# Spreading reciprocal denominators to rows by 32-row products in four parts of the array

## The chip, the cores and the metric

The kernel runs on one core of a Trainium2 chip. The metric is the device time of one execution in microseconds (us). Every time below is from the profile, its trace or the timed runs.

## What is computed

Four layers act on x, 2048 tokens of 576 numbers: linear attention (A), a feed-forward block (B), and the same two again with the same weights. Each adds its result to x. The change is in the attention layer, which has 32 heads of 18 numbers:

```
q, k, v = layernorm(x) @ wqkv, split by head
pq, pk  = phi(q), phi(k)          # phi(t) = t + 1 if t > 0 else exp(t), plus 1e-6
kv      = sum over tokens of pk (outer) v      # per head 18 x 18
z       = sum over tokens of pk                # per head 18
den     = pq . z + 1e-6                        # one number per token and head
o       = (pq @ kv) / den
x       = x + concat(o) @ wo
```

The B block is `gelu(layernorm(x) @ w1 + b1) @ w2 + b2` with 4608 hidden numbers.

## The kernel before

**Units.** Tokens stand in 16 tiles of 128 (`NT`), for the attention in 4 chunks (`NCA`) of 512 tokens (`CA`), four tiles each. The 32 heads stand in 5 groups (`G`): four of 7 heads, 126 rows, and one of 4 heads, 72 rows. `pq[(g, c)]` is phi(q) of group g and chunk c, turned: rows are the head's numbers, columns are 512 tokens.

**The attention layer (`layer_A`)** first makes the sums over all tokens, and among them queries by `q_proj` (L586), five products of 512 columns each (L589) into one PSUM buffer, which ScalarE reads twice (Exp L468, Identity L469) and VectorE completes (L476, L480). Three of the 20 `q_proj` are left for the passes 0, 1 and 2 of the output loop in layer 0, one for pass 0 in layer 2. `kv_wo` (L733) multiplies kv into wo.

**Denominators.** `den_stage(c)` (L748) makes the denominators of a chunk by products of 128 columns in four column parts of the array: rows 32j to 32j + 31 of the result are the 32 heads for tokens 128j to 128j + 127 (L755; the 1e-6 by L759). VectorE takes the reciprocal (L763) into `rden`, a single buffer. `quad_stage(c)` (L768) spreads `rden` on VectorE to `quad_rden`, 128 x 512, with a mask that leaves in each 128 columns only their own 32 rows.

**Scaling.** `scale_stage(g, c)` (L778) brings the reciprocals of a group to its rows by one product with all 128 rows and 512 columns (L783: `head_bc[:, g, :]`, a 0/1 matrix that repeats each head 18 times). ScalarE copies the result to bf16 (L785, `rden_bc`), VectorE multiplies it into `pq` (L786). The 0/1 matrix holds the same pattern once in each 32 rows.

**The output loop (L830)** runs over the 16 tiles t = 4c + j; one run of it is called a pass here. Its order is the order of TensorE, since the helper `pe` chains every product to the one before:

1. `wo_stage(t)` (L790): ten products (L795, 288 columns) of the scaled `pq` of chunk c into an accumulator pair, `accA` or `accB` in turn; VectorE adds the residual (`residual`, L519), which frees the pair for the pass after next.
2. `quad_stage` of a chunk whose reciprocal is due, and a `q_proj` if one is left.
3. `scale_stage` for the next chunk: groups 0 to 2 at j = 0, groups 3 and 4 at j = 1.
4. `den_stage(c + 2)` at j = 1.
5. `lnp.tick()`: the pipeline of row statistics for the first four tiles of the next block, on ScalarE (L337, L344) and GpSimd; from pass 6 on every second pass it transposes one of these tiles on TensorE (`tp`, L425), with a copy by ScalarE (L432).

The first chunk is scaled before the loop.

**Buffers.** PSUM has the two accumulator pairs and the pool `ps_h` of four banks. `q_proj`, `den_stage` (but for chunk 1), `scale_stage` and the transposes take their banks from `ps_h`, one each; a bank is free again when its readers are done. `turned` (L114) is an SBUF tile, 128 x 2304 in bf16, for rows on their way to be turned for the feed-forward block and, at its end, for the second attention layer; the output loop does not use it.

On ScalarE, VectorE and GpSimd the order is that of a scheduler, which mostly follows the program's, with some steps that are ready early put forward.

Of the kernel before, what the change touches and what calls it, by code (L numbers as in the profile page):

```python
# [8 lines left out]
ALU = mybir.AluOpType  # L9
BF16 = mybir.dt.bfloat16  # L10
F32 = mybir.dt.float32
# [4 lines left out]
P = 128  # L16
# [12 lines left out]
CA = 512  # L29
NCA = S // CA  # L30
# [4 lines left out]
def build(tc, A_x, A_wqkv, A_wo, B_w1, B_b1, B_w2, B_b2, out, dbg=None, n_layers=4):  # L35
    nc = tc.nc
    dbg = dbg or {}
    with ExitStack() as ctx:
        const = ctx.enter_context(tc.tile_pool(name="const", bufs=1))
        ps_h = ctx.enter_context(tc.tile_pool(name="ps_h", bufs=4, space=PSUM))  # L40
# [18 lines left out]
        head_bc = const.tile([P, G, P], BF16, name="head_bc")  # L59
# [54 lines left out]
        turned = const.tile([P, D // 32, TPC, 32], BF16, name="turned")  # L114
# [6 lines left out]
        rows = ctx.enter_context(tc.tile_pool(name="rows", bufs=9))  # L121
# [20 lines left out]
        def pe(inst):  # L142
            if pe_chain["on"]:
                if pe_chain["last"] is not None:
                    tc.add_manual_dep(inst.ins, pe_chain["last"], NOSYNC, reason="TensorE order in the MLP")
                pe_chain["last"] = inst.ins.name
            return inst
# [76 lines left out]
        dve_last = dict(norm=None, sum=None, phi=None)  # L224
# [222 lines left out]
        act_last = dict(exp=None, gelu=None)  # L447
# [14 lines left out]
        def phi_from_psum(ps_ap, out_ap, rows, n, turned_cols=False, after=None, dve_after=None, ident_after=None):  # L462
            e = work.tile([P, 512], BF16, name="phi_e", bufs=3)
            a = work.tile([P, 512], BF16, name="phi_a", bufs=2)
            e_out, a_out = e[0:rows, 0:n], a[0:rows, 0:n]
            if turned_cols:
                e_out, a_out, ps_ap = spread(e_out), spread(a_out), gather(ps_ap)
            exp = nc.scalar.activation(out=e_out, in_=ps_ap, func=ACT.Exp)  # L468
            ident_pass = nc.scalar.activation(out=a_out, in_=ps_ap, func=ACT.Identity, bias=C1, scale=1.0)  # L469
            if after is not None:  # L470
                for step in (exp, ident_pass):
                    tc.add_manual_dep(step.ins, after, NOSYNC, reason="broadcasts first")
            if ident_after is not None:
                tc.add_manual_dep(ident_pass.ins, ident_after, NOSYNC, reason="first rows first")
            act_last["exp"], act_last["phi"] = exp.ins.name, ident_pass.ins.name
            low = nc.vector.tensor_scalar(out=e[0:rows, 0:n], in0=e[0:rows, 0:n], scalar1=1.0, scalar2=1e-6,  # L476
                                          op0=ALU.min, op1=ALU.add)
            if ident_after is not None:
                tc.add_manual_dep(low.ins, dve_last["turned"], NOSYNC, reason="first rows first")
            top = nc.vector.tensor_tensor(out=out_ap, in0=a[0:rows, 0:n], in1=e[0:rows, 0:n], op=ALU.max)  # L480
            if dve_after is not None:
                tc.add_manual_dep(top.ins, dve_after, NOSYNC, reason="denominators first")
            dve_last["phi"] = top.ins.name
# [45 lines left out]
        def layer_A(li, next_kind, pre_a1=None):  # L529
# [3 lines left out]
            pq = {}  # L533
# [52 lines left out]
            def q_proj(g, c, defer=False):  # L586
                qp = ps_h.tile([P, 512], F32, name="q_ps", tag="h")
                for k in range(KD):
                    pe(nc.tensor.matmul(qp[0:GR[g], :], lhsT=wqkv_sb[:, k, GO[g]:GO[g] + GR[g]],  # L589
                                     rhs=yT[:, k, c * CA:(c + 1) * CA],  # L590
                                     start=(k == 0), stop=(k == KD - 1)))
                pq[(g, c)] = blk.tile([P, D], BF16, name="pq", tag="blk")
                phi = lambda after=None, dve_after=None: phi_from_psum(qp[0:GR[g], :], pq[(g, c)][0:GR[g], 0:CA], GR[g], CA,
                                                       turned_cols=(li > 0), after=after, dve_after=dve_after)
                if defer:
                    return phi
                phi()
# [4 lines left out]
            if li > 0:  # L602
# [87 lines left out]
                for g in range(G):  # L690
                    pe(nc.tensor.matmul(zp[0:GR[g], g:g + 1], lhsT=k2[4][:, GO[g]:GO[g] + GR[g]], rhs=ident[:, 64:65],
                                        start=True, stop=True))
# [30 lines left out]
            if li == 0:  # L723
# [5 lines left out]
                                    in1=zp[0:126, 0:4].unsqueeze(2).to_broadcast([126, 4, H]), op=ALU.mult)  # L729
            nc.vector.tensor_tensor(out=zsel[0:72, 4, :], in0=head_sel[0:72, 4, :],  # L730
                                    in1=zp[0:72, 4:5].to_broadcast([72, H]), op=ALU.mult)
# [12 lines left out]

            quad_rden = {}
            rden_of = {}

            def den_stage(c, after=None, pair=None):  # L748
                if pair:
                    dp = ps_acc.tile([P, 2, 512], F32, name="den_pair", tag=pair)[:, 0, :]  # L750
                else:
                    dp = ps_h.tile([P, 512], F32, name="den_ps", tag="h")
                for g in range(G):
                    for j in range(TPC):
                        pe(nc.tensor.matmul(dp[32 * j:32 * (j + 1), 0:P], lhsT=zsel[0:GR[g], g, :],  # L755
                                         rhs=pq[(g, c)][0:GR[g], j * P:(j + 1) * P],
                                         start=(g == 0), stop=False))
                for j in range(TPC):
                    pe(nc.tensor.matmul(dp[32 * j:32 * (j + 1), 0:P], lhsT=eps_row[:], rhs=one_row[:],  # L759
                                        start=False, stop=True))  # L760
                rden = work.tile([P, P], BF16, name="rden", bufs=1)
                with nc.allow_low_precision("reciprocal of the denominator in the reference's bfloat16"):
                    recip = nc.vector.reciprocal(out=rden[:], in_=dp[:, 0:P])  # L763
                if after is not None:
                    tc.add_manual_dep(recip.ins, after, NOSYNC, reason="first products first")
                rden_of[c] = rden

            def quad_stage(c, after=None):  # L768
                quad = blk.tile([P, D], BF16, name="quad_rden", tag="blk")
                spread_out = nc.vector.tensor_tensor(  # L770
                    out=quad[:, 0:CA].rearrange("p (j n) -> p j n", j=4), in0=quad_mask[:],
                    in1=rden_of.pop(c)[:].unsqueeze(1).to_broadcast([P, 4, P]), op=ALU.mult)
                if after is not None:
                    tc.add_manual_dep(spread_out.ins, after, NOSYNC, reason="sums first")
                quad_rden[c] = quad
                dve_last["quad"] = spread_out.ins.name

            def scale_stage(g, c, pair=None):  # L778
                if pair:
                    bp = ps_acc.tile([P, 2, 512], F32, name="rden_pair", tag=pair)[:, 0, :]  # L780
                else:
                    bp = ps_h.tile([P, 512], F32, name="rden_ps", tag="h")
                pe(nc.tensor.matmul(bp[:, 0:CA], lhsT=head_bc[:, g, :], rhs=quad_rden[c][:, 0:CA], start=True, stop=True))  # L783
                rb = blk.tile([P, D], BF16, name="rden_bc", tag="blk")
                act_last["copy"] = nc.scalar.copy(out=rb[0:GR[g], 0:CA], in_=bp[0:GR[g], :]).ins.name  # L785
                mult = nc.vector.tensor_tensor(out=pq[(g, c)][0:GR[g], 0:CA], in0=pq[(g, c)][0:GR[g], 0:CA],  # L786
                                               in1=rb[0:GR[g], 0:CA], op=ALU.mult)
                dve_last["mult"] = mult.ins.name

            def wo_stage(t):  # L790
                c, j = divmod(t, TPC)
# [28 lines left out]
            for g in range(3):  # L820
                scale_stage(g, 0)
# [8 lines left out]
            for t in range(NT):  # L830
                c, j = divmod(t, TPC)
                if t + AHEAD < NT:
                    prefetch_xo(li, t + AHEAD, add_b2=False)
                wo_stage(t)
                for late in list(rden_of):
                    quad_stage(late, after=dve_last["sum"])
                if q_left:
                    q_proj(*q_left.pop(0))
                if c + 1 < NCA:
                    for g in ((0, 1, 2), (3, 4), (), ())[j]:  # L840
                        scale_stage(g, c + 1)
                if j == 1 and c + 2 < NCA:
                    den_stage(c + 2)
                if t == NT - 3:
                    warm_table(ACT.Gelu_apprx_tanh, act_last["copy"])
                state["wo"] = t
                lnp.tick()
                if t < 10:
                    lnp.tick(transposes=0)
# [236 lines left out]
```

## Time and profile before

| what | value |
|---|---|
| median of 3 runs | 768.68 us (768.55 to 768.87) |
| the profiled execution | 768.49 us, span of its instructions 766.8 us |
| granted TensorE clock | 1.0 |
| output loop, layer 0 | from 77.69 to 107.2 us of the span |
| output loop, layer 2 | from 454.07 to 481.8 us of the span |
| L783, products that spread reciprocals | 40, one lasts 379 ns (median) |
| L785, copies of them by ScalarE | 40, 592 ns |
| L786, products on VectorE | 40, 417 ns |

How to read it: the profile holds one execution. PE is TensorE's products, PEld its weight loads, DVE is VectorE, ACT is ScalarE, POOL is GpSimd, SP starts transfers. L783 is line 783 of the kernel. A duration of a product is longer than the time after which the next may start, since they are pipelined; so starts are compared. The span is 1.7 us shorter than the time of its execution (768.49 less 766.8), and the execution 0.2 us faster than the median.

### The profile page before, as it was taken

What the parts mean: (1) busy time and instruction counts of PE and PEld (TensorE: products, weight loads), DVE (VectorE), ACT (ScalarE), POOL (GpSimd) and SP (SyncE); (2) the same over time, 40 slices, a digit from 0 to 9 for tenths busy, and PEclk for the clock granted to TensorE, in tenths of its full rate; (3) what the DMA queues carried; (4) which work ended last, traced back from release to release, by engine and by line L of the source; (5) the groups of instructions that cost most, each with busy time, mean ns of one, the idle gap of its engine ahead of it and who ended that gap; (6) DMA issues with size and microseconds to landing.
All of it is one profiled execution on the core that took longest, in us unless ns stands there. A gap on an engine that the chain in (4) does not pass through costs nothing.

```text
span 766.8 us, 15710 instructions
## 1 busy us (share of the span) xinstructions
PE 760.5 (99%) x6554; PEld 492.8 (64%) x6554; DVE 273.3 (36%) x677; ACT 338.6 (44%) x754; POOL 120.5 (16%) x196
## 2 busy tenths in 40 slices
PE   9999999999999999999999999999999999999998
PEld 6776664675477457646777767447745764674476
DVE  7786864135113603400355677600140032000000
ACT  5887856304610650164056567560065027205600
POOL 4571412011100301200100005300020021001000
PEclk9999999999999999999999999999999999999999
DMA  8992483016402721330256006630141033011000
GB/s 257 263 308 48 140 283 77 24 55 162 125 24 63 195 68 42 96 86 1 67 137 204 1 17 224 226 82 15 50 111 47 16 125 82 9 32 55 2 9 24
DMA packets 80289, 73.82 MB, mean 96 GB/s; under 512 B 36698, under 2 KB 64858, under 8 KB 80218
## 3 DMA queue, kind: packets, MB, share of 16 engines
q1 hardware_dynamic: 80218, 72.82, 32.7%
q8 instruction: 51, 0.84, 0.5%
q14 instruction: 20, 0.16, 0.1%
HBM read 48.03 MB, written 24.77 MB: 95 GB/s over the span
## 4 chain that ended last, share of the span: by engine, by line
PE 95%; ACT 3%; DVE 1%; DMA 1%; issue 1%; SPq 0%; DVEq 0%; ACTq 0%
PE m_ps L967 36%; PE h_ps L910 20%; PE hp_ps L910 16%; PE q_ps L589 5%; PE wo_ps L795 3%; PE k_ps L541 3%; PE k_ps L610 3%; PE k_ps L627 2%; PE v_ps L562 1%; PE m_half L967 1%; PE v_ps L559 1%; ACT rden_bc L785 1%; PE tp L425 1%; DMA wqkv_sb<-in_A_wqkv_dram 1%; ACT ln_dump L337 1%; PE kvacc L583 1%
## 5 line engine op out<-in xcount | busy, mean ns | idle before, releaser
L967 PE MATMUL m_ps<-w_sb,hT 128*128 128x288 bf16 x2232 | 274.8, 286 | 0.0
L967 PEld LDWEIGHTS <-hT 128*128 128x128 bf16 x2304 | 224.8, 98 | 59.8 <-issue 3.4
L910 PEld LDWEIGHTS <-w_sb 64*128 64x128 bf16 x2304 | 124.5, 94 | 136.5 <-issue 1.9
L910 PE MATMUL hp_ps<-yT,w_sb 64*128 64x512 bf16 x1152 | 178.0, 376 | 0.0
L910 PE MATMUL h_ps<-yT,w_sb 64*128 64x512 bf16 x1152 | 147.9, 376 | 0.0
L915 ACT COPY relay_sb<-relay_sb 128x1 f32<-128x1 f32 x144 | 28.5, 198 | 262.6 <-PE h_ps L910 220.0
L906 ACT ACTIVATE hT<-h_ps,b1T 128x512 bf16<-128x512 f32 x144 | 91.0, 683 | 44.4 <-PE h_ps L910 44.4
L376 POOL TENSOR_TENSOR ln_rstd<-ln_u,neg_half 128x1 f32<-128x1 f32 x64 | 36.2, 566 | 379.0 <-DVE ln_u L367 230.7
L906 ACT ACTIVATE hT<-hp_ps,b1T 128x512 bf16<-128x512 f32 x144 | 91.1, 692 | 0.0
L519 DVE TENSOR_TENSOR xbf<-m_ps,xo 128x576 bf16<-128x576 f32 x15 | 11.4, 757 | 214.0 <-PE m_ps L967 214.0
L519 DVE TENSOR_TENSOR xo<-m_ps,xo 128x576 f32<-128x576 f32 x16 | 12.1, 758 | 173.8 <-PE m_ps L967 173.8
L502 POOL TENSOR_TENSOR xo<-xo,b_bc 128x576 f32<-128x576 f32 x32 | 40.9, 1284 | 102.0 <-DMA xo<-x_d 61.9
L910 PE MATMUL h_ps<-yT,w_tail 64*128 64x512 bf16 x144 | 54.1, 376 | 0.0
L910 PE MATMUL hp_ps<-yT,w_tail 64*128 64x512 bf16 x144 | 54.1, 376 | 0.0
L589 PE MATMUL q_ps<-yT,wqkv_sb 128*126 128x512 bf16 (+1 forms) x200 | 49.8, 380 | 0.0
L795 PE MATMUL wo_ps<-kvwo,pq 126*128 126x288 bf16 (+1 forms) x320 | 43.7, 286 | 0.6 <-DVE xo L519 0.2
L910 PEld LDWEIGHTS <-w_tail 64*128 64x128 bf16 x288 | 27.1, 94 | 17.1
L795 PEld LDWEIGHTS <-pq 126*128 126x128 bf16 (+1 forms) x320 | 30.1, 97 | 11.1 <-DVE pq L786 0.8
L468 ACT ACTIVATE phi_e<-k_ps 128x288 bf16<-128x288 f32 x46 | 19.4, 421 | 38.2 <-PE k_ps L610 35.5
L468 ACT ACTIVATE phi_e<-q_ps 126x512 bf16<-126x512 f32 (+1 forms) x40 | 23.8, 596 | 19.0 <-PE q_ps L589 19.0
L589 PEld LDWEIGHTS <-wqkv_sb 128*126 128x126 bf16 (+1 forms) x200 | 24.9, 131 | 11.4
L476 DVE TENSOR_SCALAR phi_e<-phi_e 128x288 bf16<-128x288 bf16 (+2 forms) x86 | 24.1, 281 | 21.0 <-ACT phi_e L468 20.3
(135 smaller groups left out, 665.5 us busy)
## 6 DMA issues: line engine op xcount, KB each, us to landing
xo<-x_d SPq DMA_DIRECT2D x48, 288.0 KB
x_d<-xo SPq DMA_DIRECT2D x32, 288.0 KB
xl<-x_d SPq DMA_DIRECT2D x24, 288.0 KB
y_d<-turned SPq DMA_DIRECT2D x40, 144.0 KB
w_sb<-in_B_w_dram SPq DMA_DIRECT2D x6, 864.0 KB
yT<-y_d SPq DMA_DIRECT2D x10, 512.0 KB
w_sb<-in_B_w_dram SPq DMA_DIRECT2D x9, 512.0 KB
x_d<-xn SPq DMA_DIRECT2D x16, 288.0 KB
```

What stands on the lines that cost most here:

```text
L376: nc.gpsimd.tensor_tensor(out=rstd[:], in0=it["u"][:], in1=neg_half[:], op=ALU.pow)
L468: exp = nc.scalar.activation(out=e_out, in_=ps_ap, func=ACT.Exp)
L476: low = nc.vector.tensor_scalar(out=e[0:rows, 0:n], in0=e[0:rows, 0:n], scalar1=1.0, scalar2=1e-6, op0=ALU.min, op1=ALU.add)
L502: nc.gpsimd.tensor_tensor(out=xo[:], in0=xo[:], in1=b2_bc[:], op=ALU.add)
L519: total = nc.vector.tensor_tensor(out=xn[:, cols].rearrange("p (h n) -> p h n", h=2), in0=halves, in1=xo[:, cols].rearrange("p (h n) -> p ...
L541: pe(nc.tensor.matmul(kp[:, 0:HALF], lhsT=yT[:, k, tok], rhs=wqkv_sb[:, k, D + half * HALF: D + (half + 1) * HALF], start=(k == 0), stop=( ...
L589: pe(nc.tensor.matmul(qp[0:GR[g], :], lhsT=wqkv_sb[:, k, GO[g]:GO[g] + GR[g]], rhs=yT[:, k, c * CA:(c + 1) * CA], start=(k == 0), stop=(k ...
L795: pe(nc.tensor.matmul(wp[:, half, 0:HALF], lhsT=pq[(g, c)][0:GR[g], j * P:(j + 1) * P], rhs=kvwo[g][0:GR[g], half * HALF:(half + 1) * HALF ...
L906: act_last["gelu"] = nc.scalar.activation(out=to, in_=ps, func=ACT.Gelu_apprx_tanh, bias=b1T[:, f:f + 1], scale=1.0).ins.name
L910: mm = pe(nc.tensor.matmul(dst[n], lhsT=wt, rhs=mv, start=(seen[n] == 0), stop=(seen[n] == 8)))
L915: relay = nc.scalar.copy(out=relay_sb[:, 1:2], in_=relay_sb[:, 0:1])
L967: pe(nc.tensor.matmul(acc[half][:, 0:HALF], lhsT=hT[f][:, j * P:(j + 1) * P], rhs=w2_sb[:, f, half * HALF:(half + 1) * HALF], start=(f == ...
```

## The change

For the chunks 1 to 3, groups 0 to 3 are no longer scaled one by one. A new `quarter_stage(c)` takes four banks of `ps_h`, one for each 128 tokens. For each group it makes four products, one for each 32 rows of `rden` and of the 0/1 matrix (126 of its columns), each into its own bank: 16 products of 32 rows and 128 columns in place of 4 of 128 rows and 512 columns. ScalarE copies each bank whole (four groups for 128 tokens) into a quarter of `turned`; VectorE multiplies group by group, and its second operand is then four runs of 128 columns, one from each bank's copy.

Group 4 keeps `scale_stage`, and with it `quad_stage` stays. In the loop the quarter stage stands at j = 0, but at j = 1 for chunk 1 (c = 0); group 4 and `den_stage(c + 2)` follow one pass later. Chunk 0 is not touched.

```diff
             rden_of = {}
+            rden_now = {}
...
                 rden_of[c] = rden
+                rden_now["tile"] = rden
...
+            def quarter_stage(c):
+
+                rden = rden_now["tile"]
+                banks = [ps_h.tile([P, 512], F32, name="rden_ps", tag="h") for _ in range(4)]
+                for g in range(4):
+                    for i in range(4):
+                        rows = slice(32 * i, 32 * (i + 1))
+                        pe(nc.tensor.matmul(banks[i][0:126, g * P:(g + 1) * P], lhsT=head_bc[rows, g, 0:126],
+                                            rhs=rden[rows, :], start=True, stop=True))
+                spread_rows = turned[:].rearrange("p a t c -> p (a t c)").rearrange("p (i w) -> p i w", i=4)
+                for i in range(4):
+                    act_last["copy"] = nc.scalar.copy(out=spread_rows[0:126, i, 0:4 * P], in_=banks[i][0:126, :]).ins.name
+                for g in range(4):
+                    scaled = pq[(g, c)][0:126, 0:CA].rearrange("p (i n) -> p i n", i=4)
+                    mult = nc.vector.tensor_tensor(out=scaled, in0=scaled,
+                                                   in1=spread_rows[0:126, :, g * P:(g + 1) * P], op=ALU.mult)
+                    dve_last["mult"] = mult.ins.name
...
+                first = 1 if c == 0 else 0
                 if c + 1 < NCA:
-                    for g in ((0, 1, 2), (3, 4), (), ())[j]:
-                        scale_stage(g, c + 1)
-                if j == 1 and c + 2 < NCA:
+                    if j == first:
+                        quarter_stage(c + 1)
+                    if j == first + 1:
+                        scale_stage(4, c + 1)
+                if j == first + 1 and c + 2 < NCA:
                     den_stage(c + 2)
```

## The prediction

> **What bounds the kernel now.** The page first: TensorE (PE) is busy nearly the whole span, so anything it is spared counts, and anything it is made to wait for counts too.
>
> ```profile
> span 766.8 us, 15710 instructions
> ...
> PE 760.5 (99%) x6554; PEld 492.8 (64%) x6554; DVE 273.3 (36%) x677; ACT 338.6 (44%) x754; POOL 120.5 (16%) x196
> ```
>
> These shares are averages over stages. The change sits in two short ones, the output loop of each attention layer, so the second view is the busy time by stretch: passes 0 to 3, 4 to 7 and 8 to 11 of that loop, in layer 0 and then in layer 2. The columns are the stretch, its length, then busy time (instructions) of PE, PEld, DVE, ACT and POOL, the granted clock, DMA share and GB/s.
>
> ```profile
> 77.69:87.81 10.12, 10.00 (x92) 6.47 (x85) 9.04 (x22) 9.49 (x22) 1.98 (x4) 1.00 0.27 89
> 87.81:95.33 7.52, 7.20 (x77) 5.01 (x75) 6.05 (x13) 7.03 (x18) 6.37 (x14) 1.00 0.73 238
> 95.33:101.90 6.57, 6.57 (x57) 4.93 (x55) 5.19 (x10) 4.90 (x9) 1.40 (x3) 1.00 0.85 269
> 454.07:462.37 8.30, 7.99 (x80) 5.14 (x75) 8.01 (x20) 7.70 (x18) 0.45 (x2) 1.00 0.20 74
> 462.37:469.89 7.52, 7.24 (x74) 5.01 (x74) 5.69 (x12) 6.84 (x17) 6.44 (x13) 1.00 0.59 196
> 469.89:476.47 6.58, 6.58 (x56) 4.94 (x55) 5.45 (x10) 4.90 (x9) 3.25 (x7) 1.00 0.72 223
> ```
>
> In the first two stretches of each layer ScalarE (ACT) and VectorE (DVE) are nearly as full as PE; only in the third do they have room. Third view, the timeline: pass 1 of layer 0 on PE, then the load times of weights (min/median/max ns), then pass 8 of layer 2 on PE and ACT.
>
> ```profile
> 80.31 0.81 PE L783 MATMUL rden_ps<-quad_rden,head_bc 128*128 128x512 bf16 x3
> 82.19 1.24 PE L589 MATMUL q_ps<-yT,wqkv_sb 128*126 128x512 bf16 x5
> 83.27 0.59 PE L783 MATMUL rden_ps<-quad_rden,head_bc 128*128 128x512 bf16 x2
> 83.58 0.63 ACT L468 ACTIVATE phi_e<-q_ps 126x512 bf16<-126x512 f32 x1
> 83.80 0.47 PE L755 MATMUL den_ps<-pq,zsel 126*32 126x128 bf16 x20
> 84.05 0.64 ACT L469 ACTIVATE phi_a<-q_ps 126x512 bf16<-126x512 f32 x1
> 84.09 0.23 PE L759 MATMUL den_ps<-one_row,eps_row 126*32 126x128 bf16 x4
> 84.25 1.41 PE L795 MATMUL wo_ps<-kvwo,pq 126*128 126x288 bf16 x10
> ```
> ```profile
> L783 PEld LDWEIGHTS <-head_bc x40: 96/98/101, 74.0 to 473.3; 128*128 128x128 bf16 x40
> L647 PEld LDWEIGHTS <-wqkv_sb x25: 113/137/138, 427.0 to 449.3; 128*126 128x126 bf16 x20, 128*72 128x72 bf16 x5
> ```
> ```profile
> 471.12 0.81 PE L783 MATMUL rden_ps<-quad_rden,head_bc 128*128 128x512 bf16 x3
> 471.54 1.56 ACT L785 CAST rden_bc<-rden_ps 126x512 bf16<-126x512 f32 x3 [2.27 <-PE rden_ps L783]
> 471.77 0.44 PE L425 MATMUL tp<-ident,y_ring 128*128 128x128 bf16 x5
> ```
>
> Ends are modelled, so I price by starts. Three L783 products last 0.81 and one lasts 0.38: one each 0.215. Ten products of L795 (a pass) take 1.235 from start to the next work (97.48 to 98.72), a q_proj 1.08 (82.19 to 83.27), five transposes 0.28 (471.77 to 472.05).
>
> **Part 1, PE: sixteen small products for four large ones.** Removed: 4 x 0.215 = 0.86 per later chunk. The nearest row for the new products is L755: also 128 columns, four in four parts of the array (there column parts). Twenty start between 83.80 and 84.09, five batches of four: 0.058 a batch, so four batches 0.23. The array changes its partition twice. Into L755: the second L783 product ends its columns at 83.27 + 2 x 0.215 = 83.70, the next starts at 83.80: 0.10. Out: the L759 batch is through at 84.09 + 0.06 = 84.15, L795 starts at 84.25: 0.10. The first weights cannot come ahead of the change: 0.06, as before L719 (load at 70.07, product at 70.13). Sum 0.23 + 0.20 + 0.06 = 0.49; saved 0.37, over six chunks 2.2.
>
> No row shows four row parts with 126-column weights. Cheap end: both gaps hidden, 0.29. Dear end: parts take turns, each load and product like L647, whose fifteen start from 448.61 to 449.40, 0.053 to 0.058 each: 16 x 0.058 + 0.26 = 1.19, a loss of 0.33 per chunk. I take 0.49, because L910 has products in two row halves, and eight of its 512-column products take 1.04 with one at 0.38: three steps of 0.22, so they go in pairs.
>
> The weights are 126 columns wide, and the rows above show that such a load is longer (137 ns against 98). The Trainium skill (TensorE: Matmul & The Clock Gate, "Weight-path perf modes" and "LDWEIGHTS") says that only 128 columns get the fast load, and prices the others at columns / 1.2 ns; an estimate from that page is 105 ns a batch, 0.68 a stage and 0.18 saved in place of 0.37. The trace agrees on the longer load and disagrees on the price, since L647 has a load and a product every 0.058.
>
> **Part 2, four PSUM buffers at once.** ps_h has four, and the new stage takes all. In layer 0 the stage of chunk 1 stands in pass 1 right behind a q_proj, whose buffer comes free only when Exp and Identity have read it. In the trace q_proj's columns end at 82.19 + 1.08 = 83.27 and phi_a ends at 84.05 + 0.64 = 84.69: 1.4 later (1.2 if ACT is idle). PE's order is fixed, so everything waits: 1.3 after the 0.10 gap. Layer 2 has no q_proj in pass 1; that of pass 0 is read by 457.91, when PE arrives: nothing (0 to 0.2).
> At pass 8 of both layers a transpose (tp) follows. Today three products leave it the fourth buffer; now it waits for the first copy. Copy starts 0.42 after the product (471.12, 471.54; here 0.26, as the product is short), lasts 0.59 (median of L785), hand-over 0.04, less 0.10 gap and 0.06 batch: about 0.7 of waiting. Saved in that stretch: 0.37. Net **+0.3** per layer: PE had no wait there, so nothing else gives.
>
> **Part 3, the way to the scaled chunk.** Copies stay five per chunk at about 0.5 apart, products on DVE five at 0.42 (the second operand in runs of 128; L770 has such a view at 0.41; bounds 0.36 and 0.90 from L786). But a DVE product now needs all four copies, so the first starts 2.0 after the copies begin instead of 0.55, and group 4 comes a pass later, behind row statistics on ACT (L337, 0.7; L344, 0.8). Behind the waiting products on DVE stand the sums (L519, 0.75) that free the accumulators for PE's pass after next.
> - *Layer 0, passes 0 to 3.* Without three L783 products, pass 1 starts at 80.31, q_proj ends at 80.31 + 1.235 + 1.08 = 82.63, the buffer is free at about 84.05, pass 2 starts at 84.4. Then pass 2, q_proj, group 4, den and pass 3: 1.235 + 1.08 + 0.215 + 0.55 + 1.235 = 4.3, so pass 4 at 88.7, not 87.81: +0.9. Copies from 84.4 to 86.5, phi of q_proj to 87.6, copy of group 4 to 88.2 (later with statistics), DVE: four products, reciprocal 0.95, last product: about 89.6, needed at pass 4's fifth product, 88.7 + 0.49. **+1.3**.
> - *Layer 2, passes 0 to 3.* PE alone would be 0.6 earlier. ACT: phi until 457.91, statistics 0.67, copies to 460.6, statistics 1.5, copy of group 4 to 462.7; DVE's last product, behind the reciprocal, at 463.4. Pass 4's fifth product was at 462.37 + 0.49 = 462.86. **+0.5**.
> - *Passes 4 to 7.* PE's own work is 4 x 1.235 + 5 x 0.215 + 0.55 + 0.28 = 6.85 of 7.52: 0.67 is waiting, and falls with the fewer buffers in pass 5. New own work 6.48, but ACT's 7.03 and 6.84 are not reduced, and DVE's products end later. I take **-0.5** in layer 0, **-0.4** in layer 2.
>
> den_stage(2) moves from pass 1 to 2; the product it feeds in chunk 2 comes at pass 4, two passes later: no cost. The quad product on DVE stays. Copies into `turned` meet none of its DMAs, which belong to other stages; no DMA is moved.
>
> Sum: layer 0 +1.3 - 0.5 + 0.3 = +1.1; layer 2 +0.5 - 0.4 + 0.3 = +0.4; together +1.5, and +0.4 for the sums on DVE behind a run of four products: +1.9. The profiled execution took 768.49, so 770.4; the median of the runs is 0.2 higher: **770.6**.
>
> **Rivals.**
> 1. *The waits are covered and PE's saving wins (not slower).* It decides from the point where the copies reach ACT before the statistics, so that group 4 is scaled before PE's fifth product of pass 4 (layer 2: before 462.2). Then -2.2 of products and -1.3 of today's waits (0.67 in passes 4 to 7 of each layer), against 1.3 and 2 x 0.7 that remain: -0.8; with a stage at 0.29, another 6 x 0.2 less, -2.0. Time 766.7 to 767.9. For it: the third stretches have room. Against: ACT is over 90% full in the four others. Chance 0.22.
> 2. *The quarters take turns*, in the loads or in the products, so the change does not do what it says: 0.7 more per chunk, 4.2 less what already waits: 772.5 to 774.5. For it: wide slow loads, never seen in four rows. Against: L910's pairs. Chance 0.18.
> 3. *DVE's order turns bad*: the run of four products, put ahead of sums in the queue while copies are missing, holds a sum for up to 2 us per chunk: +4 to +8 more, 774 and above. Chance 0.08.
>
> Forecast (769.0 to 772.3): 0.52. A difference under 0.2%, 1.5 us, is about what a measurement here cannot tell from none. Of the forecast 0.20 lies within it, of rival 1 0.10; the rest of rival 1, 0.12, is faster. So faster 0.12, same 0.30, slower 0.58. The range 767.2 to 774.0 leaves out the fast half of rival 1 and most of rival 3.
>
> **What would show it.** L755-like batches of 0.058 in the new products and 0.49 from the last column before to the first after; a wait of PE of over 1 us on phi_a in pass 1 of layer 0; about 0.7 on the first copy before tp at pass 8; DVE products in runs of four after the fourth copy; ACT's busy time by stretch unchanged. Wrong if the first and second stretches get shorter than 10.12 and 8.30, or if the batches step by over 0.2.

## The result, and the profile after

The changed kernel takes 773.4 us (median of 4 runs, 773.01 to 773.61) against 768.62 for the kernel before in the same comparison: a ratio of 1.0061, 95% interval 1.0044 to 1.0079. It is slower by 4.8 us. The forecast was 770.6 in a range of 767.2 to 774.0: the direction and the range held, the loss was sized at 1.9 and is more than twice that.

First the page of the changed kernel, the lines that answer to those of before:

```profile
span 771.3 us, 15859 instructions
...
PE 759.3 (98%) x6626; PEld 491.9 (64%) x6626; DVE 272.3 (35%) x677; ACT 339.3 (44%) x754; POOL 119.6 (16%) x196
```

PE is busy 1.2 us less than before, in a span that is 4.5 us longer. So the small products do spare PE work, and PE now waits. The stretches of the two output loops say where (passes 0 to 3, 4 to 7, 8 to 11 of layer 0, then of layer 2; stretch, length, then busy time of PE, PEld, DVE, ACT and POOL; the cuts of two stretches lie up to 0.8 behind the first product of the pass, where the trace has a wait inside the pass):

```profile
77.23:89.13 11.90, 10.48 (x107) 6.67 (x100) 8.96 (x23) 11.27 (x26) 4.03 (x9) 1.00 0.37 122
89.13:96.85 7.72, 6.15 (x82) 4.39 (x83) 6.04 (x13) 5.50 (x13) 5.86 (x12) 1.00 0.47 159
96.85:104.16 7.31, 6.40 (x67) 4.89 (x67) 4.80 (x10) 5.21 (x9) 0.00 (x0) 1.00 0.72 226
456.33:465.00 8.67, 8.19 (x97) 5.19 (x89) 6.78 (x17) 8.04 (x19) 2.13 (x5) 1.00 0.21 72
465.00:473.69 8.69, 6.93 (x85) 4.74 (x86) 7.67 (x15) 6.71 (x16) 6.79 (x15) 1.00 0.73 220
473.69:481.00 7.31, 6.41 (x68) 4.89 (x68) 4.79 (x10) 5.21 (x9) 0.37 (x1) 1.00 0.84 263
```

The third stretches, in which PE waited for nothing before (6.57 of 6.57, 6.58 of 6.58), now hold 0.9 us of waiting each. What PE waited for in the loops, layer 0 and then layer 2 (total us, times, longest):

```profile
PE rden_ps L799 <- ACT phi_a L469: 1.2, 1, 1.2
PE wo_ps L815 <- DVE pq L788: 1.1, 1, 1.1
PE wo_ps L815 <- DVE xn L519: 0.8, 2, 0.6
PE tp L425 <- ACT turned L803: 0.7, 1, 0.7
```
```profile
PE wo_ps L815 <- DVE xo L519: 1.8, 3, 1.4
PE tp L425 <- ACT turned L803: 0.7, 1, 0.7
PE rden_ps L785 <- ACT turned L803: 0.2, 1, 0.2
```

L799 is the new product, L803 the copy of a bank, L806 the VectorE product of a group, L815 the old L795, L785 the spreading product that group 4 keeps, L788 its VectorE product, L764 the reciprocal; L519 is the sum, which adds the residual (xn in layer 0, xo in layer 2). In the runs further down the line numbers are shifted; the names of the tiles tell which instruction it is. The kernel before had such waits of 0.2 twice in the two loops.

To compare kernels I use the length of the loops, from the first L795 (or L815) product to the first product of the feed-forward block, since the start-up of one execution moves by up to 0.9 us (the loop of layer 0 begins at 77.69 before, at 77.23 after, and from 77.14 to 78.06 in the other runs). "Fifth product" is the one of a pass that needs group 4.

| from the loop's first product, us | layer 0: pass 4 fifth | pass 8 fifth | end | layer 2: pass 4 fifth | pass 8 fifth | end |
|---|---|---|---|---|---|---|
| before | 10.61 | 18.12 | 29.51 | 8.79 | 16.31 | 27.71 |
| after | 12.89 | 20.11 | 32.24 | 9.32 | 17.84 | 29.97 |
| difference | +2.28 | +1.99 | +2.73 | +0.53 | +1.53 | +2.26 |

The loops are 4.99 longer together, which is the whole loss (4.8 by the medians).

Three places of the changed kernel's timeline show how. Pass 1 of layer 0, on PE and ACT:

```profile
82.26 0.27 PE L799 MATMUL rden_ps<-rden,head_bc 32*126 32x128 bf16 x3
82.61 0.58 ACT L468 ACTIVATE phi_e<-q_ps 126x512 bf16<-126x512 f32 x1
83.08 0.59 ACT L469 ACTIVATE phi_a<-q_ps 126x512 bf16<-126x512 f32 x1
83.72 0.39 PE L799 MATMUL rden_ps<-rden,head_bc 32*126 32x128 bf16 x13 [1.19 <-ACT phi_a L469]
```

Three of sixteen products go, the fourth needs the bank that the q_proj just filled, and PE stands until ACT has read it twice. Pass 8 of layer 0:

```profile
98.17 0.45 PE L799 MATMUL rden_ps<-rden,head_bc 32*126 32x128 bf16 x16
98.69 2.05 ACT L803 CAST turned<-rden_ps 126x512 bf16<-126x512 f32 x4 [2.93 <-PE rden_ps L799]
99.33 0.44 PE L425 MATMUL tp<-ident,y_ring 128*128 128x128 bf16 x5 [0.71 <-ACT turned L803]
```

The transpose waits for the first of the four copies. Passes 6 to 8 of layer 2, DVE and then PE:

```profile
469.85 1.97 DVE L806 TENSOR_TENSOR pq<-pq,turned 126x512 bf16<-126x512 bf16 x4 [0.54 <-ACT turned L803]
471.75 0.41 DVE L788 TENSOR_TENSOR pq<-pq,rden_bc 72x512 bf16<-72x512 bf16 x1
472.08 0.94 DVE L764 RECIPROCAL rden<-den_ps 128x128 bf16<-128x128 f32 x1
472.95 0.69 DVE L519 TENSOR_TENSOR xo<-wo_ps,xo 128x576 f32<-128x576 f32 x1
473.69 1.39 PE L815 MATMUL wo_ps<-kvwo,pq 126*128 126x288 bf16 x10 [1.42 <-DVE xo L519]
```

Pass 6 was through on PE when tp began at 470.60. Its sum, which frees the accumulator for pass 8, starts at 472.95, behind four products, the fifth and the reciprocal.

### The profile page after: what moved, and what is told of

Read it like the earlier page. It is cut to its first block, busy times and chain, and to the rows that moved or that the text cites. A ratio compares the mean times of both kernels' runs of the same rounds, so it can differ in the third digit from the quotient of the medians.

```text
span 771.3 us, 15859 instructions
## 1 busy us (share of the span) xinstructions
PE 759.3 (98%) x6626; PEld 491.9 (64%) x6626; DVE 272.3 (35%) x677; ACT 339.3 (44%) x754; POOL 119.6 (16%) x196
## 5 line engine op out<-in xcount | busy, mean ns | idle before, releaser
L519 DVE TENSOR_TENSOR xbf<-m_ps,xo 128x576 bf16<-128x576 f32 x15 | 11.4, 757 | 215.1 <-PE m_ps L990 215.1
L519 DVE TENSOR_TENSOR xo<-m_ps,xo 128x576 f32<-128x576 f32 x16 | 12.1, 758 | 174.3 <-PE m_ps L990 174.3
L815 PE MATMUL wo_ps<-kvwo,pq 126*128 126x288 bf16 (+1 forms) x320 | 44.5, 286 | 4.0 <-DVE xo L519 1.8
L815 PEld LDWEIGHTS <-pq 126*128 126x128 bf16 (+1 forms) x320 | 29.8, 97 | 14.8 <-issue 3.0
```

The source lines that it names most:

```text
L519: total = nc.vector.tensor_tensor(out=xn[:, cols].rearrange("p (h n) -> p h n", h=2), in0=halves, in1=xo[:, cols].rearrange("p (h n) -> p ...
L815: pe(nc.tensor.matmul(wp[:, half, 0:HALF], lhsT=pq[(g, c)][0:GR[g], j * P:(j + 1) * P], rhs=kvwo[g][0:GR[g], half * HALF:(half + 1) * HALF ...
```

## The experiments

Two theories went in. **All at once**: taking four banks together makes the neighbours in PE's order wait, and four VectorE products in a run behind the fourth copy hold the sums; the small products themselves are cheap. **Late**: the move alone costs, with group 4 and the denominators a pass later. Later a third stood against the first for passes 4 to 7: VectorE is simply full there. The times of runs are medians; beside each stands its ratio to the kernel before, with a 95% interval. The kernel before had 768.4 to 768.6 in these comparisons.

### Old products at the new places

```diff
                     if j == first:
-                        quarter_stage(c + 1)
+                        for g in range(4):
+                            scale_stage(g, c + 1)
```

> Edit: the old scaling products (128 rows, 512 columns) stand at the new places, groups 0 to 3 in one pass, group 4 and the denominators a pass later. 'All at once' (four banks taken together, and four VectorE products in a run behind the fourth copy, are what costs; the small products themselves save 0.38 per chunk): the waits of 1.5 and 0.7 get shorter, the products cost 2.3 more: 770.0 to 772.0. 'Late' (the move of group 4 and of the denominators alone is what costs): nothing is mended and the saving is lost, 773.4 + 2.3 = 775.7, at least 774.5.

Measured 770.17, ratio 1.0022 (1.0012 to 1.0031). The loops are 1.52 (layer 0) and 0.35 (layer 2) longer than before. So the move is no innocent: behind a q_proj, the fourth of four products waits for a bank here as well, 0.7 us, and PE waits 0.9 us for group 4 in pass 4 of layer 0. But that is 1.9 of the 5.0, and "late" fails as the whole cause: the kernel with the small products, which has 2.3 us less work for PE, is 3.1 us longer. By the length of passes that is 1.8 in pass 7 (the sum for pass 8), 0.7 in pass 10 (the sum for pass 11), 0.6 in pass 2 of layer 2 and 0.4 in pass 8, less 0.4 elsewhere.

### The order within a pass

```diff
+                if t == 2 * TPC:
+                    state["wo"] = t
+                    lnp.tick()
+                if c + 1 < NCA and j == first:
+                    quarter_stage(c + 1)
                 if q_left:
                     q_proj(*q_left.pop(0))
...
```

> Edit: the changed kernel, with the quarter stage ahead of q_proj in a pass, and in pass 8 the transpose ahead of it. 'All at once': the transpose no longer waits, 2 x 0.7 gone; the wait of 1.5 in pass 1 of layer 0 becomes one of about 0.6 for q_proj; 773.4 - 1.4 - 0.9 = 771.1, and up to 772.0 where VectorE's sums are late instead. 'Late': no bank wait is behind it, 773.0 to 773.6.

Measured 774.42, ratio 1.008 (1.0065 to 1.0095): slower than the change and outside the ranges of both theories. PE's waits in layer 0:

```profile
PE q_ps L589 <- ACT turned L803: 1.6, 1, 1.6
PE wo_ps L815 <- DVE xn L519: 1.3, 2, 0.9
PE wo_ps L815 <- DVE pq L788: 0.9, 1, 0.9
PE rden_ps L799 <- ACT yT L432: 0.6, 1, 0.6
```

The waits changed places. A stage that takes all four banks makes whoever stands behind it wait for a copy (now the q_proj, 1.6, because two row statistics stood ahead of the copies on ACT), and waits itself for whoever stands before it (now the transpose's copy, L432). Turning the order round within a pass cures nothing. That the waits move with the order speaks for the banks and against "late", though it mended nothing.

### The neighbours moved to other passes

```diff
-                    lnp.feed(xn, t, "B", "pool", "act", hold=1, stats="act", tp_at=6 + 2 * t)
+                    lnp.feed(xn, t, "B", "pool", "act", hold=1, stats="act", tp_at=7 + 2 * t)
...
-                if q_left:
+                if q_left and (t != 1 or li > 0):
                     q_proj(*q_left.pop(0))
```

> Edit: the changed kernel with its neighbours moved away: the q_proj of pass 1 in layer 0 comes in pass 3, the transposes in passes 7, 9, 11, 13. 'All at once', if the bank waits cost by themselves: the waits of 1.5 (layer 0) and 2 x 0.7 go, 773.4 - 2.8 = 770.6. If what they delayed is held by VectorE anyway (the run of products and the sums), the first is not won: 772.0 to 772.8.

Measured 770.60, ratio 1.003 (1.0018 to 1.0041). The loops are 30.49 and 29.06, 2.66 shorter than with the change; the bank waits were 1.45 (from the third to the fourth of the new products in pass 1 of layer 0), 0.7 and 0.7, together 2.9. By parts of the loop the account is less smooth. Up to the fifth product of pass 4 layer 0 wins 1.50, a little more than the wait. From there to the fifth product of pass 8 it loses 0.65 again, since the sum that pass 8 needs is late: PE waits 1.1 for it, where it waited 0.6. From there to the end each layer wins 0.90, the bank wait and a part of the one for a sum. So the bank waits cost by themselves, but in layer 0 VectorE took back nearly half of the first one, and that the total comes near 2.9 is partly chance. Whether the q_proj that now stands in pass 3 adds to that late sum, this run can't tell. What remains, 2.3 over before, is mostly not the banks; PE's waits in layer 0, then in layer 2:

```profile
PE wo_ps L815 <- DVE xn L519: 1.1, 1, 1.1
PE wo_ps L815 <- DVE pq L788: 0.6, 1, 0.6
PE q_ps L589 <- ACT turned L803: 0.3, 1, 0.3
...
PE wo_ps L815 <- DVE xo L519: 1.6, 2, 1.4
PE rden_ps L785 <- ACT turned L803: 0.3, 1, 0.3
```

3.3 of these 3.9 are waits for VectorE, 0.6 for banks.

### Chunk 1 the old way

```diff
-                    if j == first:
+                    if c == 0:
+                        for g in ((0, 1, 2), (3, 4), (), ())[j]:
+                            scale_stage(g, c + 1)
+                    elif j == 0:
                         quarter_stage(c + 1)
...
```

> Edit: chunk 1 is scaled the old way at the old places, chunks 2 and 3 as in the changed kernel. From the two traces, the fifth product of pass 4 is 2.3 later in layer 0 and 0.5 later in layer 2 against the first product of the loop. 'All at once', with each chunk costing its own: 773.4 - 2.8 = 770.6. If the losses of passes 4 to 7 are only the tail of the late pass 4, more goes: 769.0 to 769.8. If they come anyway once VectorE is full (its load does not change), less goes: 771.5 and above.

Measured 771.17, ratio 1.0033 (1.002 to 1.0046); loops 30.82 and 29.20, 2.19 shorter than with the change. Up to the fifth product of pass 4 the loops are as before to 0.01. The loss of passes 4 to 8 is not the tail of a late pass 4: the fifth product of pass 8 is 0.57 and 0.76 later than before all the same. Each chunk has a cost of its own.

### The sums first

```diff
+                if 0 < c < NCA - 1 and j in (1, 2):
+                    for g in ((0, 1), (2, 3))[j - 1]:
+                        quarter_mult(g, c + 1, after=dve_last["sum"])
```

The products of chunks 2 and 3 leave the stage and stand two by two behind the sums of the next two passes (`quarter_mult` is the product of L806 with an order behind the named sum).

> Edit: the changed kernel, but for chunks 2 and 3 the four VectorE products do not run in a row: two stand behind the sum of the next pass, two behind that of the pass after. 'All at once': PE's waits for sums (0.6 and 1.4 in pass 8, 0.36 twice in pass 11) go, 773.4 - 2.7 = 770.7, to 771.8 if the reciprocal still holds a sum. Rival 'VectorE is simply full in passes 4 to 7': the order of its work does not matter, 773.0 to 773.8.

Measured 772.86, ratio 1.0055 (1.0038 to 1.0071): loops 0.65 shorter than with the change, where 2.7 were expected; the time lies between the ranges of the two theories. Pass 7 is 0.7 shorter in both layers and pass 10 0.36, as expected; but pass 8 is 0.65 longer, since PE now waits for the last two products of chunk 2. In passes 4 to 7 these two products could not be moved behind a sum without being late themselves; in passes 8 to 11 it cost 0.08 in pass 12 for 0.36 won.

### Chunk 3 alone

The edit is shown against the loop of the kernel before, with `quarter_stage` added above it.

```diff
+                if c == 2:
+                    if j == 0:
+                        quarter_stage(c + 1)
+                    if j == 1:
+                        scale_stage(4, c + 1)
-                if c + 1 < NCA:
+                elif c + 1 < NCA:
                     for g in ((0, 1, 2), (3, 4), (), ())[j]:
                         scale_stage(g, c + 1)
```

> Edit: only chunk 3 (pass 8) goes by the quarter stage, with the four VectorE products in a run; chunks 1 and 2 as before. ACT and VectorE have room there, so only two costs are left: the transpose waits for the first copy, and the sum of pass 9 stands behind the run. From the changed kernel's trace the stretch of passes 8 to 11 is 0.74 longer in each layer: 768.6 + 1.5 = 770.1. If that loss were inherited from the late passes before it, 767.8 to 768.6.

Measured 769.57, ratio 1.0016 (1.0007 to 1.0025); the loops are 0.69 longer in each layer, and the loss of this stretch is its own.

The next three runs take that apart. First, with the transposes on odd passes (`tp_at=7 + 2 * t`, as above) and the products two by two behind the sums of passes 9 and 10:

```diff
-                        quarter_stage(c + 1)
+                        quarter_stage(c + 1, mults=False)
...
+                    for g in ((), (0, 1), (2, 3), ())[j]:
+                        quarter_mult(g, c + 1, after=dve_last["sum"])
```

> Edit: only chunk 3 goes by the quarter stage, its VectorE products stand two by two behind the sums of passes 9 and 10, and the transposes move from passes 6, 8, 10, 12 to 7, 9, 11, 13, away from the stage. 'All at once': nothing waits for the four banks and no sum is held, so the saving is kept, 2 x 0.38: 768.6 - 0.8 = 767.8. If the small products cost more than the trace shows, or the waits come back elsewhere: 768.6 to 770.

Measured 767.92, ratio 0.9995 (0.9987 to 1.0004). The stretch of passes 8 to 11 in the trace, layer 0 and layer 2:

```profile
95.55:101.74 6.19, 6.19 (x69) 4.78 (x68) 4.72 (x10) 5.08 (x8) 1.40 (x3) 1.00 0.85 279
469.74:475.93 6.19, 6.19 (x68) 4.78 (x68) 4.66 (x10) 4.99 (x8) 3.10 (x7) 1.00 0.64 203
```

PE busy all of 6.19 where it was busy all of 6.57 and 6.58: the saving of 0.38 per chunk, kept whole. The loops are 29.13 and 27.33, 0.76 shorter than before. The runs' times, whose interval takes in 1, cannot show so small a gain; the two traces agree on it in both layers.

The control, the kernel before with the transposes on odd passes alone:

```diff
-tp_at=6 + 2 * t)
+tp_at=7 + 2 * t)
```

> Edit: the kernel before with the transposes in passes 7, 9, 11 and 13 alone, the control for the run with chunk 3. All theories: 768.6, within 0.3, as PE's work is the same and the transposed tiles are due only behind pass 15.

Measured 768.65, ratio 1.0003 (0.9994 to 1.0012), loops 29.52 and 27.71: nothing.

And the run of four VectorE products put back, with the transposes still on odd passes:

```diff
-                        quarter_stage(c + 1, mults=False)
+                        quarter_stage(c + 1)
...
-                        quarter_mult(g, c + 1, after=dve_last["sum"])
```

> Edit: on the run with chunk 3 alone, the four VectorE products are put back into a run, with the transposes still on odd passes. 'The run holds the sum of pass 9': PE's wait of 0.36 comes back in each layer, 767.9 + 0.7 = 768.6. If only the transposes mattered: 767.9.

Measured 768.26, ratio 0.9996 (0.9987 to 1.0006); loops 29.32 and 27.51, 0.19 and 0.18 more, in pass 11 (1.69 for 1.51). The times are too close to show it; the traces do. VectorE in passes 9 to 11 of layer 0:

```profile
98.65 0.76 DVE L519 TENSOR_TENSOR xn<-wo_ps,xo_pair 128x576 f32<-128x576 f32 x1 [0.96 <-PE wo_ps L821]
99.39 1.43 DVE L795 TENSOR_TENSOR pq<-pq,turned 126x512 bf16<-126x512 bf16 x4
100.73 0.41 DVE L788 TENSOR_TENSOR pq<-pq,rden_bc 72x512 bf16<-72x512 bf16 x1
101.07 1.41 DVE L519 TENSOR_TENSOR xn<-wo_ps,xo_pair 128x576 f32<-128x576 f32 x2
```

The run does hold a sum, by half of the 0.36 expected, but not the one that was named. The sum of pass 9 (98.65) goes ahead of the run, since no transpose holds up pass 9 any more; the sum of pass 10 (the first of the two at 101.07) stands behind it, and pass 12, which needs its accumulator, begins 0.18 late at 101.87. With the transposes on even passes the sum of pass 9 stood behind the run, and pass 11 began 0.36 late. So of the 1.08 per layer between the two versions of chunk 3, the transposes account for 0.89 and the order of the VectorE products for 0.19.

### Chunk 2 with the reciprocal out of the way

```diff
+                elif c == 1:
+                    if j == 0:
+                        quarter_stage(c + 1)
+                    if j == 1:
+                        scale_stage(4, c + 1)
...
-                if j == 1 and c + 2 < NCA:
+                if j == 1 + c and c + 2 < NCA:
                     den_stage(c + 2)
```

The base is the kernel with chunk 3 alone and transposes on odd passes. The reciprocal of pass 6 is ordered behind that pass's sum.

> Edit: on the run with chunk 3 alone (767.9), chunk 2 goes by the quarter stage too, with its four VectorE products in a run, but the denominators of chunk 3 come in pass 6 instead of 5 and their reciprocal stands behind the sum of pass 6. In the run with chunk 1 the old way, passes 4 to 8 were 0.57 and 0.76 longer than before, and PE waited 0.5 and 0.9 for that sum. 'The sum behind the run and the reciprocal is the cost': 767.9 + 0.57 + 0.76 - 1.4 = 767.8 (767.4 to 768.2). 'VectorE is simply full in passes 4 to 7': taking the reciprocal out of the way only moves the wait, 768.8 to 769.4.

Measured 768.03, ratio 0.9993 (0.9984 to 1.0003); loops 29.47 and 27.26. In layer 2 the fifth product of pass 8 comes at 16.25, before it was 16.31; in layer 0 at 18.46, before 18.12. VectorE in passes 5 to 8 of layer 2:

```profile
466.85 1.43 DVE L797 TENSOR_TENSOR pq<-pq,turned 126x512 bf16<-126x512 bf16 x4 [1.08 <-ACT turned L814]
468.20 0.41 DVE L790 TENSOR_TENSOR pq<-pq,rden_bc 72x512 bf16<-72x512 bf16 x1
468.54 0.75 DVE L519 TENSOR_TENSOR xo<-wo_ps,xo 128x576 f32<-128x576 f32 x1
469.20 0.95 DVE L764 RECIPROCAL rden<-den_ps 128x128 bf16<-128x128 f32 x1
```

L797 is the product of a group here, L790 that of group 4. The sum now goes ahead of the reciprocal, and PE's wait for it falls from 0.9 to 0.2. Moving the transposes alone had not done that: in the run with the neighbours moved, layer 2 still waited 1.4 for this sum. "VectorE is simply full" fails in layer 2: it even idles 1.08 before the run, for the fourth copy. In layer 0 a wait of 0.5 for the sum stays, and in both layers group 4's product still waits 0.4 to 0.6 for a bank. So in layer 2 the wait for the sum was a matter of order, mostly; but the saving of chunk 2 is not won. Against the base the loops are 0.06 shorter in layer 2 and 0.34 longer in layer 0, where 0.38 was to be had in each.

What makes the run late is ScalarE: its copies begin 1.62 after the first product of the stage in layer 2 (463.19 to 464.81) and 1.76 in layer 0 (88.68 to 90.44), behind row statistics, where chunk 3 waited 0.47 in the base (96.87 to 97.34). In layer 0 the first product of the run also takes 0.63 for 0.43. No run took the statistics out of the way.

### The price of the products

```diff
-                        pe(nc.tensor.matmul(banks[i][0:126, g * P:(g + 1) * P], lhsT=head_bc[rows, g, 0:126],
+                        pe(nc.tensor.matmul(banks[i][:, g * P:(g + 1) * P], lhsT=head_bc[rows, g, :],
```

> Edit: on the run with chunk 3 alone, the 16 products take all 128 columns of the 0/1 matrix instead of 126. If the longer load of 126 columns is behind the first batch (0.10 where the later ones take 0.057), the load falls from 130 to 97 ns and the first batch to 0.06: the stage from 0.476 to 0.43 in the trace; in time 0.1, not to be seen. If the first batch is long for another reason, the stage stays at 0.476.

From the traces, the base (chunk 3 alone, its VectorE products behind the sums) first, then the wide weights; load times (min/median/max ns), then the stage on PE (L808, and L821, the output products behind it):

```profile
L808 PEld LDWEIGHTS <-head_bc x32: 127/131/133, 96.9 to 471.2; 32*126 32x126 bf16 x32
...
471.06 0.45 PE L808 MATMUL rden_ps<-rden,head_bc 32*126 32x128 bf16 x16
471.43 0.54 PE L821 MATMUL wo_ps<-kvwo,pq 126*128 126x288 bf16 x3
```
```profile
L808 PEld LDWEIGHTS <-head_bc x32: 90/93/94, 96.9 to 471.2; 32*128 32x128 bf16 x32
...
471.05 0.40 PE L808 MATMUL rden_ps<-rden,head_bc 32*128 32x128 bf16 x16
471.39 0.54 PE L821 MATMUL wo_ps<-kvwo,pq 126*128 126x288 bf16 x3
```

The load falls from 131 to 93 ns, and the time from the first product to the next work from 379 to 335 ns. Two columns of zeros more are faster, by about the 0.04 us that a load is shorter: the second batch starts 106 ns after the first in the base and 67 ns here, while the later batches follow each other at 56 to 58 ns in both, so only one load is not hidden behind products.

The second edit turns the two loops of the stage round:

```diff
-                for g in range(4):
-                    for i in range(4):
+                for i in range(4):
+                    for g in range(4):
```

> Edit: on the run with chunk 3 alone, the 16 products go part by part (four groups in one part of the array, then the next part) instead of group by group. If products are handed out in order and only neighbours in the queue overlap, three of four steps wait for their own part: 16 products at about 0.058 less the three changes of part, 0.7 to 0.9 instead of 0.23, the stage at 1.0 to 1.2, and passes 8 to 11 longer by 0.5 to 0.7 in each layer. If the parts drain queues of their own, the stage stays at 0.48.

The stage on PE:

```profile
470.59 0.48 PE L808 MATMUL rden_ps<-rden,head_bc 32*126 32x128 bf16 x16
471.00 0.91 PE L821 MATMUL wo_ps<-kvwo,pq 126*128 126x288 bf16 x6
```

Sixteen products, four after each other for the same part, take 409 ns to the next work instead of 379. Had they started in the queue's order, a part's four would have gone one after another and only the last of one part beside the first of the next: 13 steps of 0.057, 0.74. So the parts work off their products beside each other in either order. The single records agree. The queue holds the product that completes a bank, and signals it, as its fourth, eighth, twelfth and sixteenth; the four records that signal are the last four to start, 221, 234, 248 and 261 ns after the first. The starts go in batches of four as in the base, 13 ns apart within a batch where they were 3 to 4. That the parts have queues of their own is inferred from this; the records do not name the part.

## Why the prediction was right or wrong

The direction was forecast for the right kind of reason: PE is spared work and then made to wait for banks and for VectorE. That the range held is in part luck. The measured 773.4 lies outside the band of the forecast itself (769.0 to 772.3) and inside that of rival 2 (772.5 to 774.5), whose mechanism did not happen.

**Part 1, PE's price: right.** Predicted 0.49 a stage and 0.37 saved; measured 0.38 saved (6.57 and 6.58 to 6.19). By the price of a load in the Trainium skill (TensorE: Matmul & The Clock Gate, "LDWEIGHTS"), its columns / 1.2 ns, the estimate of the saving was 0.18; the measured 0.38 decides for the price taken from the trace's row. The Trainium skill (TensorE: Matmul & The Clock Gate, "Weight-path perf modes") gives the fast load to weights of 128 columns; the trace agrees, 93 ns against 131 with 126, but that is worth 0.04 a stage. Rival 2, that the quarters take turns, fell: the batches step by 0.057.

**Part 2, the banks: right.** Predicted 1.3 in pass 1 of layer 0 and 0.7 at pass 8 of both; the trace has 1.45 between the starts of the third and fourth product, 1.19 of it marked idle, and 0.71 twice. Taken away together they gave 2.66, with 0.65 of the first lost again to a late sum and some of the last two due to sums. What the step left out is a third place: group 4's product a pass later also finds all banks taken (0.2 to 0.6).

**Part 3 was mis-sized, in two terms.** Against the terms of the sum, each as lengthening of the loop:

| term | predicted | measured |
|---|---|---|
| layer 0, to the fifth product of pass 4 | +1.3 | +2.28 |
| layer 2, the same | +0.5 | +0.53 |
| passes 4 to 7, layer 0 | -0.5 | -0.29 |
| passes 4 to 7, layer 2 | -0.4 | +1.00 |
| pass 8 to the end, each layer | +0.3 | +0.74, +0.73 |
| sums behind the run of products | +0.4 | in the terms above |

The mis-sized step is the one for VectorE's order. The prediction had a sum held behind a run as a lump of 0.4 in all, and as rival 3, up to 2 us per chunk, at a chance of 0.08. Measured in passes 7 and 10 of the changed kernel, it is 0.36 in each third stretch and 0.6 and 1.4 before pass 8, 2.7 together. So the mechanism of rival 3 is the one that happened (one sum, in layer 2, was 2 us late), but smaller than its +4 to +8. For passes 4 to 7 the prediction took it that today's 0.67 of waiting falls with the fewer buffers of pass 5, and let only ACT's load, which is not reduced, limit the gain. The load was not the point: in layer 2 VectorE stood idle until the fourth copy and then had four products, a fifth and a reciprocal ahead of a sum that was due 2 us earlier.

In pass 4 of layer 0 the prediction let the group-4 product follow the reciprocal, 0.9 too early: it also stood behind a phi step and the sum of pass 3, and its copy came 0.7 later, behind statistics on ACT.

**Rival 1** (the waits are covered) fell for the change as it is. It holds for chunk 3 once its neighbours are moved.

What stays open: whether chunk 2 keeps its saving once the row statistics on ACT no longer stand ahead of its copies, and what chunk 1 could give, whose stage stands only three passes ahead of its use. Of chunk 1's cost in layer 0, 2.28, the bank wait is shown (1.50 comes back without it); the rest, group 4's late copy and product, is read from the timeline alone. A version in which each bank holds one group, so that every copy frees a VectorE product at once, was not tried.

The best version that was timed more than once is chunk 3 alone with the transposes on odd passes and its VectorE products behind the sums: 0.76 less in the loops, 767.92 against 768.43, and by the runs not distinguishable from before. The weights of 128 columns take another 0.02 to 0.03 per layer off its loops, in the one trace there is.

## What to carry to other kernels

A step that makes an engine's work cheaper by taking a whole pool at once has to be priced with its neighbours in that engine's order: who gave back the last buffer, and who wants the first. And if four results become ready together instead of one after another, look at what stands behind their consumers on the next engine, above all what frees the accumulators of the bottleneck: the load may be the same, and the order still cost more than the saving. Try such a change first where the other engines have room, and move what collides to other passes.

## What the runs showed of the hardware

- Four products of 32 rows and 128 columns in four row parts took 0.057 us a batch, with weights of 126 columns loaded for each; sixteen took 0.34 to 0.41 us to the next work, the change of partition on the way out included.
- Queue order hardly mattered for them: part by part cost 0.03 us more than batch by batch.
- A 32-row load of 128 columns took 93 ns, of 126 columns 131 ns (L808): dropping two columns of zeros made the load longer.
- A VectorE product whose second operand lies in four runs of 128 cost what the contiguous one did: 420 ns (L806, median) against 417 (L786).
